# Merging sorted runs by falling-gap stages instead of pairwise rounds, with the gathers put in another order

## The chip, the cores and the metric

The kernel runs on one core of one Trainium2 chip. The metric is the device time of one execution, in microseconds. The engines are named as the profile names them: PE multiplies matrices, DVE is the vector engine, ACT the scalar engine, POOL is GpSimd, SP issues most of the plain transfers.

## The reference

One GraphSAGE layer on a random graph of N = 12,500 nodes, E = 800,000 edges and D = 64 features:

```python
def reference(x, src, dst, deg_inv, w_self, w_neigh):
    N = x.shape[0]
    nsum = _segment_sum(x[src], dst, N)
    h_neigh = nsum * deg_inv[:, None]
    return x @ w_self + h_neigh @ w_neigh
```

## The kernel before

The kernel turns the gather and the segment sum into matrix multiplications with one-hot matrices. For that, edges must stand in buckets: a bucket is a pair of a block of 156 destinations and a block of 128 sources, 7,938 in all.

**Keys and runs.** Each edge becomes one 32-bit key, with its bucket in the upper bits, that is compared as a float. Each of the 128 partitions sorts its own 6,250 keys (`sort_runs`): a stage compares places a fixed gap apart, with one `min` and one `max` on DVE over every second place and a small ACT copy of the unpaired places; the gaps fall from 2601 to 1 (`GAPS`). The last 26 stages are done in three segments, low, middle and high keys.

**Gathering runs.** The sorted keys are written to DRAM. `find_rows` counts in each run where each range of buckets starts (256 counts, on ACT or on DVE by `on_act`). From the starts, POOL gathers with indirect transfers (`gather_runs`, L461): the ranges go to partitions, and each partition then holds 128 short runs, 64 keys wide in part 0 (38 buckets to a partition) and 48 in part 1 (25 buckets). Behind each gather stand one or two small fills on POOL (`pause`, L374).

**Merging.** `merge_runs` merges the 128 runs of a partition pair by pair in seven rounds (`merge_round`, L274 and L286; the last round of part 0 is `merge_last`, L303 and L318), in the order of the gathers: 16, 16, 32 and 64 runs for part 0. `LENS` holds the length that a merged run may have at each level. The last round of part 0 finishes the lower 2,240 places first.

**Windows and decoding.** The merged row goes to DRAM. `count_below` counts for each bucket where it begins, and POOL gathers a window of 186 keys around that place (`gather_window`, L621). For part 0, `find_buckets` counts all 38 buckets while the upper keys are finished, and `gather_buckets` then gathers the 38 windows. `decode_buckets` splits the keys into source and destination numbers (L668 to L673) and collects what does not fit (L707 to L722).

**The node loop.** `nodes` goes over 7,938 buckets in tiles of eight. For each bucket DVE makes two one-hot matrices (`one_hots`, L798 and L801), PE picks features with one (L827), ACT moves them out of PSUM (L837; from tile 503 on DVE takes some, L835), and PE adds them up with the other (L882).

**Order.** From the run sort on, the order is written by hand (`tc.manual_schedule()`): every engine gets its instructions in the order of the Python statements, and each engine's queue is served in order. `merge_runs` is a generator that yields the estimated cost of every DVE instruction, so that other work can be put between. Part 0 is merged before the loop. Part 1 is merged partly in `sums_and_merge` between the steps of the decode of part 0 (2,800 ns to a step), and the rest inside the loop at 320 ns a tile. After it, still inside the loop, part 1 is counted, gathered and decoded.

Of the kernel before, what the change touches and what calls it, by code (L numbers as in the profile page):

```python
# [38 lines left out]
LENS = ((64, 108, 188, 336, 608, 1144, 2176, 4320),  # L39
        (48, 80, 132, 236, 420, 780, 1472, 2912))  # L40
LROW = [l[-1] for l in LENS]
FIRST = 104
EXT = 29
SIDE = H + EXT
PITCH2 = [l + 2 * SIDE for l in LROW]
# [7 lines left out]
SHARED = 100  # L53
# [4 lines left out]
SIGMA = 6.0  # L58
LOWER = 2240
CLOSE = 32  # L60
BEHIND = 6
# [51 lines left out]
NLOWER = sum(lo + n <= LOWER for lo, n in WIN.w2[0])  # L113
NC1 = len(WIN.w1)


def on_act(c):

    return c % 13 in (0, 2, 4, 7, 9, 11) or c < 128 or c >= 128 + SHARED
# [7 lines left out]
def constants():  # L127
# [6 lines left out]
    assert max(lo + 2 * n for lo, n in WIN.w1[:128]) + LENS[0][0] <= SPLITS[1]  # L134
# [4 lines left out]
    for p in range(2):  # L139
# [11 lines left out]
        c2[:, 4] = first + np.arange(128)[:, None] * PITCH2[p]  # L151
# [8 lines left out]


def reach(k, n, total=None):

    i = np.arange(max(n - k, 0))
    m = 2.0 * i + k + 1
    var = m * (total - m) / total if total else m
    i = i[(k + 1.0) ** 2 <= SIGMA ** 2 * var]
    return (int(i[0]), int(i[-1]) + 1) if len(i) else (0, 0)  # L170


def distances(n, total=None):

    out = []
    k = 1
    while k < n:
        lo, hi = reach(k, n, total)
        if hi > lo:
            out.insert(0, (k, lo if lo > 3 else 0, hi))  # L180
        k *= 2
    return out
# [62 lines left out]
def merge_plan(ln, lout):  # L245

    out = []
    c = lout  # L250
    for k, lo, hi in reversed(distances(ln)):
        out.insert(0, (k, lo, min(hi, c // 2), min(hi, (c + 1) // 2 - k)))
        alone = (0, lo + k), (hi + k, (c + 1) // 2), (ln, ln + lo), (ln + hi, ln + c // 2)
        c = min(2 * ln, c + 2 * k - 1)
    return out, (c + 1) // 2, c // 2, [(a, e) for a, e in alone if e > a]


def merge_round(nc, src, oth, off, rstride, nruns, ln, lout, late):

    plan, na, nb, alone = merge_plan(ln, lout)
    n2 = nruns // 2

    def at(t, first, n, step=1):
        return view(t, off + first, [[2 * ln, n2], [step, n]])

    def both():
        for a, e in alone:
            nc.scalar.activation(at(src, a, e - a), at(oth, a, e - a), AF.Copy)  # L270

    for op, n, to in ((OP.min, na, 0), (OP.max, nb, ln)):
        x, y = (view(src, off + o, [[2 * rstride, n2], [1, n]]) for o in (0, rstride))
        nc.vector.tensor_tensor(at(oth, to, n), x, y, op=op)  # L274
        yield n2 * n / 0.96 + 125
    cur, nxt = oth, src
    for j, (k, lo, *ends) in enumerate(plan):
        if not j and not late():
            both()
        for op, end, z in zip((OP.min, OP.max), ends, (1, 2 * k)):  # L280
            n = end - lo
            if k == 1:
                to = at(nxt, 2 * lo + z, n, 2)
            else:
                to = at(nxt, ln + lo if op == OP.min else lo + k, n)
            nc.vector.tensor_tensor(to, at(cur, ln + lo, n), at(cur, lo + k, n), op=op)  # L286
            if not j and op == OP.min and late():
                both()
            yield n2 * n / 0.96 + 125
        cur, nxt = nxt, cur  # L290


def merge_last(nc, src, oth, off, rstride, ln, lout, split, done):


    plan, na, nb, alone = merge_plan(ln, lout)

    def at(t, z, n):
        return view(t, off + z, [[2, n]])
# [11 lines left out]
    for upper in range(2):  # L311
# [10 lines left out]
        if not upper:  # L322
            done(cur)
# [861 lines left out]
```

## Time and profile before

| | |
|---|---|
| time, median of 3 runs | 2043.04 us (2041.74 to 2045.15) |
| profiled execution | 2042.86 us, span 2041.1 us |
| DVE busy | 1862.6 us (91%) |
| ACT busy | 1216.7 us (60%) |
| PE busy | 1001.6 us (49%) |
| POOL busy | 770.4 us (38%) |
| first min of the high segment | 347.4 us |
| last min or max of the merge of part 0 ends | 801.8 us |
| first decode of part 0 | 833.5 us |
| first one-hots of the loop | 930.5 us |
| last merge instruction of part 1 begins | 1402.8 us |

The busy shares are averages over two very different halves. In the first, up to about 930 us, keys are sorted, merged and decoded and PE has almost nothing to do; in the second the node loop runs. A busy share is read within its half.

### The profile page before, as it was taken

Reading aid. Unit: us, or ns where it says so; the run is one execution under the profiler, and the core shown is the slowest. Engines: PE = TensorE matmul, PEld = TensorE weight load, DVE = VectorE, ACT = ScalarE, POOL = GpSimd, SP = SyncE. Lnnn points to the kernel's source line nnn. Section 1 sums busy time; section 2 is a strip of 40 time slices with the busy share of each in tenths; the row PEclk is TensorE's granted clock in tenths of the full one; section 3 lists DMA queues with packets and bytes.
Section 4 is the critical chain, followed back from the end, with each engine's and each line's share of the span. In section 5 each row is a group of like instructions: output and inputs, shape, how many; then the busy total and the mean of one; then the engine's idle time right before and its main releaser. Section 6 shows DMA issues by size and latency. Waiting matters only on the chain.

```text
span 2041.1 us, 56578 instructions
## 1 busy us (share of the span) xinstructions
PE 1001.6 (49%) x24532; PEld 878.6 (43%) x24532; DVE 1862.6 (91%) x2077; ACT 1216.7 (60%) x1802; POOL 770.4 (38%) x973
## 2 busy tenths in 40 slices
PE   0031000000000000005989989998866989989987
PEld 0031000000000000004777878787765878878876
DVE  7999999999999999998999999999998988887885
ACT  6371018470100005224998999998865877877886
POOL 1000000288988898783221321232622123232330
PEclk9976555555555555556999999999987999999998
DMA  4231000011010001217787887888765887887884
GB/s 150 56 89 37 0 26 15 4 50 23 20 19 14 14 10 53 61 43 219 247 273 261 272 256 255 261 265 294 240 208 179 280 266 252 270 275 256 249 264 145
DMA packets 105865, 314.90 MB, mean 154 GB/s; under 512 B 52306, under 2 KB 60340, under 8 KB 104968
## 3 DMA queue, kind: packets, MB, share of 16 engines
q1 hardware_dynamic: 87256, 287.07, 39.9%
q0 software_dynamic: 17776, 22.06, 8.7%
q8 instruction: 193, 3.16, 0.6%
q10 hardware_dynamic: 576, 2.08, 0.3%
q14 instruction: 64, 0.52, 0.1%
HBM read 291.97 MB, written 19.18 MB: 152 GB/s over the span
## 4 chain that ended last, share of the span: by engine, by line
DVE 39%; PE 38%; issue 9%; POOL 7%; ACT 5%; DMA 2%; DVEq 0%; SPq 0%; ACTq 0%; POOLq 0%
PE ct L827 21%; PE acc L882 15%; DVE u L286 11%; DVE a L224 8%; DVE b L224 7%; POOL u L461 4%; DVE u L274 2%; DVE ohd L801 2%; DVE u L318 2%; POOL v L621 2%; DVE ohs L798 2%; ACT xg L837 2%; POOL pad L374 1%; DVE junk L600 1%; PE po L946 1%
## 5 line engine op out<-in xcount | busy, mean ns | idle before, releaser
L837 ACT ACTIVATE xg<-ct 128x1024 f16<-128x1024 f32 (+1 forms) x929 | 877.9, 1051 | 167.2 <-PE ct L827 155.9
L827 PE MATMUL ct<-xh,ohs 128*128 128x128 f16 x7938 | 567.2, 226 | 60.0 <-issue 25.2
L827 PEld LDWEIGHTS <-ohs 128*128 128x128 f16 x7938 | 473.0, 101 | 100.2 <-issue 36.2
L461 POOL DMA_INDIRECT u<-d,ix x256 | 335.4, 1310 | 386.4 <-DVE ix L453 345.3
L286 DVE TENSOR_TENSOR u<-u 128x256 f32<-128x256 f32 (+47 forms) x494 | 452.9, 948 | 23.3 <-ACT u L270 16.2
L882 PE MATMUL acc<-ohd,xg 64*128 64x78 f16 x15876 | 422.1, 201 | 74.8 <-issue 41.8
L882 PEld LDWEIGHTS <-xg 64*128 64x128 f16 x15876 | 337.9, 97 | 144.0 <-issue 64.7
L846 POOL DMA_INDIRECT lx<-xt,lsrc x139 | 232.2, 1671 | 370.0 <-PE acc L862 315.4
L801 DVE TENSOR_TENSOR ohd<-iota,dlT 128x2184 f16<-128x2184 bf16 x284 | 366.3, 1290 | 0.0
L798 DVE TENSOR_SCALAR ohs<-slb,pidx 128x3584 f16<-128x3584 bf16 x284 | 327.4, 1153 | 31.5 <-PE ct L827 28.0
L688 PE MATMUL tr<-idb,l 128*128 128x128 bf16 x63 | 8.6, 278 | 453.2 <-ACT l L682 450.9
L270 ACT ACTIVATE u<-u 128x256 f32<-128x256 f32 (+15 forms) x94 | 46.4, 567 | 283.2 <-DVE u L274 283.1
L688 PEld LDWEIGHTS <-l 128*128 128x128 bf16 x63 | 5.2, 121 | 455.8 <-ACT l L682 454.6
L224 DVE TENSOR_TENSOR a<-b 128x764 f32<-128x764 f32 (+39 forms) x104 | 171.5, 1692 | 3.8
L224 DVE TENSOR_TENSOR b<-a 128x764 f32<-128x764 f32 (+39 forms) x104 | 171.5, 1691 | 3.6
L954 POOL DMA_DIRECT2D out<-o x26 | 25.2, 971 | 351.6 <-DVE o L953 257.9
L835 DVE CAST xg<-ct 128x1024 f16<-128x1024 f32 x70 | 85.6, 1223 | 76.8 <-PE ct L827 76.5
L451 PE MATMUL stp<-idf,st 128*128 128x128 f32 x2 | 0.9, 445 | 283.4 <-DVE st L449 283.4
L451 PEld LDWEIGHTS stp<-idf,st 128*128 128x128 f32 x2 | 0.4, 183 | 283.9 <-issue 283.9
L621 POOL DMA_INDIRECT v<-d,ix x63 | 79.9, 1269 | 76.8 <-ACT ix L651 49.4
L442 ACT ACTIVATE junka<-b,c 128x220 bf16<-128x220 f32 (+42 forms) x202 | 90.1, 446 | 12.0 <-DVE b L224 6.0
L374 POOL MEMSET pad<- 128x93 f32 x454 | 87.7, 193 | 9.4
(140 smaller groups left out, 813.5 us busy)
## 6 DMA issues: line engine op xcount, KB each, us to landing
slb<-sl SPq DMA_DIRECT2D x284, 896.0 KB
u<-d,ix POOLq DMA_INDIRECT x256, 2.7
xt<-xh SPq DMA_DIRECT2D x1, 3136.0 KB
own<-os SPq DMA_DIRECT2D x12, 256.0 KB
fo<-own SPq DMA_DIRECT2D x26, 117.0 KB
out<-o POOLq DMA_DIRECT2D x26, 117.0 KB, 3.4
lx<-xt,lsrc POOLq DMA_INDIRECT x139, 6.8
rd<-dst SPq DMA_DIRECT2D x4, 521.0 KB
```

The source lines that it names most:

```text
L224: nc.vector.tensor_tensor(view(dst, lo + sh, [[st, g], [1, l]]), x, y, op=op)
L286: nc.vector.tensor_tensor(to, at(cur, ln + lo, n), at(cur, lo + k, n), op=op)
L374: self.nc.gpsimd.memset(self.pad, 0.0)
L442: nc.scalar.activation(junks[0][:, :n], w, AF.Sign, bias=self.c1[:, 0, c:c + 1], accum_out=a)
L461: nc.gpsimd.indirect_dma_start(out=u[:nr, p * w:(p + 1) * w], out_offset=None, in_=src, in_offset=bass.IndirectOffsetOnAxis(ap=self.start[ ...
L621: self.nc.gpsimd.indirect_dma_start(out=self.v[:, k].bitcast(F32), out_offset=None, in_=flat(self.d2[part], 128 * PITCH2[part]), in_offset ...
L798: nc.vector.tensor_scalar(s.rearrange("p c s -> p (c s)"), b, self.pidx[:, :1], None, op0=OP.is_equal)
L801: nc.vector.tensor_tensor(d, self.iota[:, None].to_broadcast([128, 14, HN, 2]), ix, op=OP.is_equal)
L827: nc.tensor.matmul(ct[:, i * 128:(i + 1) * 128], cols[i][0], self.xh[:, (b0 + i) % NB].rearrange("p a f -> p (a f)"), start=True, stop=True)
L837: nc.scalar.activation(xg[:, :cnt * 128], ct[:, :cnt * 128], AF.Copy)
L846: nc.gpsimd.indirect_dma_start(out=x, out_offset=None, in_=self.xt, in_offset=bass.IndirectOffsetOnAxis(ap=self.left[p][1][:, c:c + 1], ax ...
L882: nc.tensor.matmul(acc[h][:, db % OCT * HN:(db % OCT + 1) * HN], xg[r, i * 128:(i + 1) * 128], d[r], start=db % OCT == 0 and sb == 0, stop ...
```

## The change

- The seven pairwise rounds go. The runs of a block of 32 are written interleaved, key r of run q at place 32 r + q, and sorted by `near` stages of falling gaps (193 to 31 in part 0, each gap twice); then the four blocks are interleaved and sorted by `far` stages (169 down to 1). A stage is one `min`, one `max` and, where places are unpaired, small ACT copies. `lens` holds how far each stage needs to reach. The blocks are merged as 64, 32 and 32 runs.
- The last 20 stages of part 0 finish the lower 2,240 places first, then the upper ones. The lower 18 windows are counted and gathered while the upper places are sorted, from a DRAM tensor of their own; the other 20 windows come from a second one. Their indices are computed on ACT, one by one.
- The remaining 49 counts of part 0 stand before the high segment instead of between its stages, 27 of them on DVE, and the gathers of part 0 start there, with no pause. Of part 1's counts, 60 instead of 100 stand before the merge; the other 68 come at two of three merge instructions.
- POOL gathers 80 runs of part 1, then the lower windows, 16 more runs, the upper windows, and the last 32 runs. Before it was 104 runs, all windows, 24 runs. The two pauses after each gather of part 1 stay.

```diff
+MERGE = (((193, 133, 89, 65, 51, 31), (169, 131, 73, 49, 31, 27, 15, 13, 9, 7, 5, 3, 3, 1, 1, 1, 1),
+          (2048, 1968, 1816, 1652, 1564, 1464, 1396, 1356, 1320, 1284, 1272, 1256, 5000, 4760, 4672, 4612)),
+         ((225, 133, 71, 59, 53), (201, 109, 55, 49, 31, 23, 19, 15, 13, 9, 5, 5, 3, 3, 1, 1, 1),
+          (1536, 1432, 1380, 1232, 1176, 1088, 1020, 980, 936, 912, 3624, 3392, 3336, 3236, 3196, 3144, 3100)))
+PAUSE = (0, 2)
-FIRST = 104
+FIRST = 80
+THEN = 96
-SHARED = 100
+SHARED = 60
+LAST = 20
...
 def on_act(c):
-    return c % 13 in (0, 2, 4, 7, 9, 11) or c < 128 or c >= 128 + SHARED
+    if c < 128:
+        return c < NEARLY or (c - NEARLY) % 9 in (0, 2, 4, 6)
+    return c >= 128 + SHARED or c % 2 == 0
...
     def gather_runs(self, part, u, runs):
...
-            self.pause(1 if part == 0 and p >= CLOSE else 2)
+            self.pause(PAUSE[part])
...
     def merge_runs(...):
+        def first(b, nb, gap, end):
+            a, rows = gap // 32, end // 32
+            dims = lambda c: [[n, nb], [2 * w, 16], [1, c]]
+            outs = lambda c: [[n, nb], [2, 16], [32, c]]
+            copy(b * n + w, b * n + 1, dims(a), outs(a))
+            copy(b * n + w - a, b * n + 32 * (w - a), dims(rows - w + a), outs(rows - w + a))
+            yield from pair(b * n, b * n + w + a, dims(0), (b * n, (outs(0), min(w - a, rows))),
+                            (b * n + gap, (outs(0), min(w, rows) - a)))
...
+        def stage(b, nb, gap, odd, last, end, low, cut):
+            o = b * n
+            one = lambda c: [[n, nb], [2, c]]
+            inside = gap < EDGE and last == end
+            if not inside:
+                for a, c in (every2(1 - odd, min(gap + odd, end), low, cut),
+                             every2(last - gap + (last - gap - odd) % 2, end, low, cut)):
+                    copy(o + a, o + a, one(c), one(c))
+            a, c = every2(odd, end if inside else min(last - gap, end), low, cut)
+            h, k = every2(1 - odd if inside else gap + odd, end, low, cut)
+            for op, out, x, count in ((OP.min, a, a, c), (OP.max, h, h - gap, k)):
+                d = [[n, nb], [2, count]]
+                if count > 0:
+                    nc.vector.tensor_tensor(view(dst, EDGE + o + out, d), view(src, EDGE + o + x, d),
+                                            view(src, EDGE + o + x + gap, d), op=op)
+                    yield cost(count * nb)
...
     def after_sort(self, es, mps, aps):
...
+            for _ in rows:
+                pass
+            self.gather_runs(0, u0, range(128))
+            for step in high:
                 step()
...
-            for _ in self.merge_runs(0, u[0], other, (16, 16, 32, 64)):
-                if rows and next(rows, None) is None:
+            ways = None
+            for i, _ in enumerate(self.merge_runs(0, u0, other, ((0, 2), (2, 1), (3, 1)))):
+                if rows and (i % 3 != 2) and next(rows, None) is None:
                     rows = None
                     self.l1b.close()
-                    self.gather_runs(1, u[1], range(FIRST))
+                    self.gather_runs(1, u1, range(FIRST))
...
+                if self.lower and not ways:
+                    vp = va.enter_context(tc.tile_pool(name="va", bufs=1, side="right"))
+                    self.windows(0, vp)
+                    self.store_rows(0, sync)
+                    ways = self.find_and_gather(0, range(NLOWER), 1)
+                elif ways and i % 2:
+                    next(ways, None)
+            for _ in ways:
+                pass
+            self.store_rows(1, sync)
+            self.gather_runs(1, u1, range(FIRST, THEN))
...
     def sums_and_merge(...):
+        for _ in self.find_and_gather(0, range(NLOWER, KPRS[0]), 1):
+            pass
+        self.gather_runs(1, u1, range(THEN, 128))
+        merge = self.merge_runs(1, u1, other, ((0, 2), (2, 1), (3, 1)))
         t = 0
         for k in self.decode_buckets(0, self.v, vp, mps):
             t += 2800
             while t > 0 and k < KPRS[0]:
                 t -= next(merge)
```

More of the change, by code (lines that the diff above doesn't have):

```diff
@@ L242, in sort_runs @@
     return cur, segments
[L245 to L290, printed above, removed]
@@ new lines, in merge_runs @@
+        na = 2 * len(near)
+        for b, nb in blocks:
+            src, dst = u, pong
+            for t in range(na):
+                gap, end = near[t // 2], lens[t]
+                if t:
+                    yield from stage(b, nb, gap, t % 2, lens[t - 1], end, 0, n)
+                else:
+                    yield from first(b, nb, gap, end)
+                src, dst = dst, src
+        src, dst = u, pong
+        yield from joined(far[0], lens[na - 1], lens[na])
+        src, dst = dst, src
```

286 lines of the change are left out of this document (112 added, 174 removed).

## The prediction

> **What bounds the kernel now.** I read the busy shares by slice first, then the engines over stretches, then the timelines of DVE and POOL.
>
> ```profile
> span 2041.1 us, 56578 instructions
> ...
> PE   0031000000000000005989989998866989989987
> ...
> DVE  7999999999999999998999999999998988887885
> ...
> POOL 1000000288988898783221321232622123232330
> ```
>
> A slice is 51 us. Up to slice 18 (about 930 us) DVE is full and PE empty: keys are sorted, merged and decoded there. After it PE is full: the node loop. POOL is nearly full in slices 7 to 17, with the gathers of runs and windows.
>
> ```profile
> core 0: us, PE busy (x) PEld busy (x) DVE busy (x) ACT busy (x) POOL busy (x), PEclk, DMA share, GB/s
> 347.40:412.50 65.10, 0.45 (x1) 0.18 (x1) 62.21 (x56) 33.46 (x126) 17.26 (x23) 0.50 0.05 16
> 440.00:801.80 361.80, 0.45 (x1) 0.18 (x1) 341.49 (x386) 53.11 (x146) 322.80 (x509) 0.50 0.09 19
> 833.40:930.50 97.10, 5.87 (x38) 3.24 (x38) 90.37 (x132) 21.45 (x42) 87.15 (x133) 0.50 0.25 66
> 932.00:1400.00 468.00, 417.02 (x10557) 367.40 (x10555) 442.25 (x478) 419.85 (x477) 110.29 (x65) 0.95 0.81 259
> 1400.00:1566.00 166.00, 126.82 (x3039) 110.42 (x3037) 158.53 (x220) 126.89 (x169) 60.24 (x51) 0.89 0.70 232
> 1566.00:2000.00 434.00, 391.00 (x9972) 345.29 (x9974) 360.67 (x401) 339.30 (x369) 118.20 (x78) 0.95 0.82 261
> ```
>
> These are: the high segment of the run sort; the merge of part 0; the decode of part 0; then the loop while part 1 merges, while part 1 is counted and decoded, and afterwards. DVE sets the first three, but POOL is busy for 323 of the 362 us of the merge and 87 of the 97 us of the decode. Whoever shortens DVE's work there meets POOL next. That is my whole forecast: DVE's saving is real and POOL's queue takes it back.
>
> **DVE's prices, and the new merge.**
>
> ```profile
> 392.73 2.42 DVE L224 TENSOR_TENSOR a<-b 128x1057 f32<-128x1057 f32 x2
> 395.19 2.43 DVE L224 TENSOR_TENSOR b<-a 128x1057 f32<-128x1057 f32 x2
> L224 DVE TENSOR_TENSOR a<-b 128x764 f32<-128x764 f32 x26 | 23.7, 952 | 0.4
> L224 DVE TENSOR_TENSOR a<-b 128x3100 f32<-128x3100 f32 x2 | 6.7, 3386 | 0.1
> ```
>
> The last two rows give (3386 - 952) / (3100 - 764) = 1.042 ns an element. The first two start 2.46 us apart for two instructions, so 1.23 us each, 0.13 above the 1.10 of the elements. These stages already step over every second element, as the new merge's do, so the price carries over.
>
> I count instructions from the code. The old plan of part 0 is 370 instructions on 287,188 elements: 299 + 48 = 347 us. A new stage is one min and one max over every second place; the second near stage of part 0 (gap 193, end 1968), for one block, is 927 and 887 elements. Added up, part 0 is: near 72 instructions on 70,544 elements, 83 us; far up to the split 28 on 61,607, 68 us; lower 40 on 45,292, 52 us; upper 40 on 41,108, 48 us. Sum 251 us, 96 less. Part 1 falls from 212 instructions on 193,080 elements (229 us) to 128 on 144,716 (167 us). The ACT copies of unpaired places (up to 226 elements) run beside the stage and cost nothing while ACT is as free as in these stretches (53 of 362 us). In the loop they queue behind ACT's evacuations, and DVE's next stage, and the one-hots behind it, wait for them.
>
> ```profile
> DVE u L286 <- ACT u L270: 16.2, 16, 2.1
> ```
>
> That is the whole of such waiting over 1,200 us of old merges, so I take nothing; if that cover goes, the 30 or so stages with copies at its longest wait of 2.1 are 60 us of DVE, of which the loop, PE-bound, would see a part. The indices that move from DVE to ACT, the edge fills, the third window tensor and the lower windows' counts on ACT lie beside DVE's stages or its waits: nothing.
>
> **POOL's prices.**
>
> ```profile
> 596.18:812.20 216.02, 154.76 (x104) 0.50 0.09 22
> 886.20:930.50 44.30, 30.27 (x24) 0.50 0.21 59
> 823.40:886.20 62.80, 3.65 (x24) 2.07 (x24) 59.53 (x101) 14.91 (x28) 56.81 (x76) 0.50 0.27 69
> 714.00 13.22 DVE L286 TENSOR_TENSOR u<-u 128x1152 f32<-128x1152 f32 x10
> 715.36 2.07 POOL L461 DMA_INDIRECT u<-d,ix  x1 [0.15 <-issue]
> 717.43 0.42 POOL L374 MEMSET pad<- 128x93 f32 x2
> 718.01 2.09 POOL L461 DMA_INDIRECT u<-d,ix  x1 [0.15 <-issue]
> 412.57 0.43 DVE L444 TENSOR_SCALAR_CACHE_REDUCE junkd<-b,c 128x214 bf16<-128x214 f32 x1
> 412.89 0.95 POOL L461 DMA_INDIRECT u<-d,ix  x1 [0.15 <-issue]
> 592.29 0.95 POOL L461 DMA_INDIRECT u<-d,ix  x1 [0.16 <-issue]
> 593.59 0.95 POOL L461 DMA_INDIRECT u<-d,ix  x1 [0.16 <-issue]
> ```
>
> A gather takes 0.95 us beside DVE's counts and 2.07 beside its min and max: in the rows at 714 to 718 DVE's instructions are 1.32 us apart and gathers with two pauses 2.65, two DVE instructions. I read it so: a gather that meets a running min or max goes on only when that ends, and then needs some 0.8 us more. With the two pauses (0.42 and gaps) it has just missed the next boundary, and waits for the one after. So a gather with two pauses costs two DVE instructions (2.4 to 2.6 us) beside stages of 1.2 to 1.3 us, and 0.95 + 0.42 + gaps = 1.53 when DVE stands still. The stretch of 104 such gathers averages 2.08, the last 24 (beside the decode) 1.85. The 38 windows, with one pause, average 62.8 / 38 = 1.65; a pause and its gap are 0.35 (the two last rows start 1.30 apart), so 1.30 without. A gather without pause is in no row. It is at least 0.95 and, by the last two rows, at most 1.30 beside an idle DVE; I take 1.10 (0.95 and one issue gap of 0.15), and beside min and max one per DVE instruction, if that lasts over 1.1 us, else one per two.
>
> **The path to the node loop, in order.** All times are from the start of the span; the old high segment starts at 347.4.
>
> ```profile
> L442 ACT ACTIVATE junka<-b,c 128x220 bf16<-128x220 f32 (+42 forms) x202 | 90.1, 446 | 12.0 <-DVE b L224 6.0
> L442 ACT ACTIVATION_READ_ACCUMULATOR junka<-b,c 128x1 f32 x202 | 38.0, 188 | 0.0
> L444 DVE TENSOR_SCALAR_CACHE_REDUCE junkd<-b,c 128x213 bf16<-128x213 f32 (+50 forms) x54 | 21.5, 398 | 1.9
> ```
>
> 1. The 49 late counts of part 0 now stand before the high segment: 27 on DVE at 0.44 (between the 0.40 of the row and 0.48 with its accumulator read) are 12 us, 22 on ACT at 0.63 are 14, and ACT enters some 1.5 us late. The starts are there at about 365 instead of 392.5, and the high segment runs from 365 to 429 instead of to 412.5.
> 2. The upper counts before the merge fall from 100 to 60, on DVE from 54 to 30: 13 us, to 442.
> 3. The 128 gathers of part 0 run from 365: 52 beside the 52 instructions of the high segment, 12 in the 13 us of counts, so the 64 of the first two blocks have landed at about 444 (2.7 us to landing). A block is a quarter of the near elements, 17,636: the pair of blocks has 24 near instructions of 1,470, 1.66 us each, and ends at 484; 24 more gathers fit. Eight of block 2 are missing: 8 x 1.10, DVE waits 9 us. Block 2 has 24 of 0.89 us and ends at 514; 12 or 13 fit, 19 are missing, DVE waits 20. Block 3 ends at 556.
> 4. Far 68: 623 or 624. Lower to 676, upper to 724. Before: 801.8.
> 5. Here it turns. 60 counts were done up front; the other 68 come at two of three merge instructions, so the starts of part 1 are worked out after the 102nd, two instructions into the lower stages: 626. POOL's queue then gets 80 gathers of part 1 with two pauses, and only behind them the 18 lower windows. Twenty fit beside the lower stages (50 / 2.6), twenty beside the upper (48 / 2.4), the last forty take 1.53: 61 us. They end at 785. The lower windows were to be gathered while the upper keys are sorted; they are ready to, but stand behind these 80.
> 6. DVE's next instruction after the merge is the decode of windows 0 to 3, ahead of any merge of part 1. Four windows at 1.10 and a landing: 792. DVE stands still from 724 to 792, 68 us. Before, that decode began at 833.4, so 41 us are still ahead.
> 7. POOL goes on: 38 windows at 1.30 (49 us) and 48 gathers of part 1, between 1.53 and the 1.85 of the row, at 1.7 (82 us): 916, landed at 919. The merge paced into the decode is 20 steps of 2.8 us; the pair of blocks and block 2 use up 40 of those 56, and then DVE waits for the last run, inside the decode. Behind it lie 17 us of merge, two groups of decode (4) and the last steps (L707 to L722, 10): 950.
>
> ```profile
> 920.24 4.73 DVE L722 MAX8 top<-e 128x8 f32<-128x138 f32 x16
> 930.51 1.17 DVE L798 TENSOR_SCALAR ohs<-slb,pidx 128x3584 f16<-128x3584 bf16 x1 [2.10 <-DMA slb<-sl]
> ```
>
> 8. From the end of the MAX8 at 925.0 to the first one-hot at 930.5 are 5.5 us, and that stays: the loop starts at about 955, 24.5 late.
>
> **The loop.** 24 matmuls of a tile of eight columns: 10,557 in 468 us are 1.064 us a tile while merging, 9,972 in 434 us 1.045 afterwards. The merge costs the loop 2%, since PE is the bound either way. Left at its start are now 66 instructions, 110 us by the code's own cost; at 320 ns a tile that is 343 tiles.
>
> ```profile
> 930.00:1404.00 474.00, 145.04 (x131) 0.95 0.81 260
> L835 DVE CAST xg<-ct 128x1024 f16<-128x1024 f32 x70 | 85.6, 1223 | 76.8 <-PE ct L827 76.5
> ```
>
> Before, 131 instructions last to 1404, some 440 tiles. Ninety-seven tiles at 0.019 less: 2 us. The stretch of counts and decode did 3,039 / 24 = 127 tiles in 166 us, against 132 for them at 1.045: it loses 34 us to DVE, which is busy for 158.5 of it. It keeps its work, but now ends near tile 440, before tile 503, where casts on DVE begin; some eight or nine casts of 1.22 leave it. I take half, 5 us.
>
> **Sum.** The profiled execution took 2042.9 (span 2041.1 and 1.8 around it; the median of the runs is 2043.0). 2042.9 + 24.5 - 2 - 5 = 2060. About 0.2% (4 us) is what a measurement of this kernel can tell from no change.
>
> **Rivals.**
> *Gathers slip through; faster.*
>
> ```profile
> 669.92 6.12 DVE L286 TENSOR_TENSOR u<-u 128x1384 f32<-128x1384 f32 x4
> 671.38 0.96 POOL L461 DMA_INDIRECT u<-d,ix  x1 [0.15 <-issue]
> 672.92 0.95 POOL L461 DMA_INDIRECT u<-d,ix  x1 [0.15 <-issue]
> ```
>
> Here gathers kept DVE's pace of 1.53 and none waited, so the outcome hangs on phase. If the 128 gathers of part 1 average 1.6, step 5 ends at 754 and step 7 at 754 + 42 + 77 + 3 = 876, the loop starts at 912, and with step 3's waits at 10 instead of 29 us at 893: 2042.9 - 37.5 - 7 = 1998. The forecast's own average is (159 + 82) / 128 = 1.88; it takes about 1.75 to cancel the loss (17.5 us / 128 less). Against it: 2.08 over 104.
> *Unpaused gathers crowd out DVE; slower still.* The same lack of pauses could make each gather hold DVE up. At 0.4 us for 128 gathers, or at 1.65 a gather instead of 1.1 to 1.23, step 3 ends 40 to 50 us later and everything behind it: about 2105. For it: nobody has shown them without pause. Against it: DVE's 13.22 us for ten instructions above are 1.32 each, the plain price, with four to five gathers running. The Trainium skill (SBUF — State Buffer, Who interferes with whom) has a VectorE instruction with two SBUF inputs and a GpSimd one that reads SBUF lock each other out, and the first to start blocks the other for its whole length; by its second half each gather could cost DVE up to its 0.95 us, 122 us for part 0, and the sum would be some 2180. The trace agrees that the gather waits; that DVE waits for the gather it does not show.
> *It cancels.* If DVE bounds the loop more than I think (34 us of loss halved, the merging tiles at 1.045), the loop gives back 20 to 25: 2043.
>
> **How the numbers follow.** Forecast (2040 to 2085) 0.50, slip-through (1985 to 2035) 0.25, crowding (2085 to 2125) 0.13, cancelling (2030 to 2047) 0.12. Faster: 0.25, and 0.05 of cancelling and 0.04 of the forecast's low end, 0.34. Same: 0.05 of cancelling and 0.03 of the forecast, 0.08. Slower 0.58. The range 2000 to 2098 leaves out the lower third of slip-through and about the upper two thirds of crowding, 0.17.
>
> **What would show it.** In the profile after: merge instructions of part 0 at 180 and some 251 us; first window gather near 785 behind 80 gathers; DVE idle 60 to 75 us before the first decode, released by POOL; a second long wait of DVE in the decode, for the last runs; first one-hot near 955. I am wrong if windows start under 750, if gathers of part 1 average under 1.7, or if block 3 starts after 560.

## The result, and the profile after

The changed kernel takes 2112.4 us (median of 4 runs, 2102.0 to 2117.4) where the kernel before takes 2042.4 on the same chip: a ratio of 1.0335, 95% interval 1.0288 to 1.0381. It is slower, as forecast, by 70 us instead of 17. The profiled execution took 2116.9 us with a span of 2114.9. First its busy shares by slice.

```profile
span 2114.9 us, 56184 instructions
...
PE   0051000000000000000788989887788998899997
...
DVE  7999999925899950646999999989968887788885
...
POOL 1000001778102988882213213334222132133231
```

A slice is now 53 us. DVE was full from slice 1 to the loop; now it has holes in slices 8 and 9 and again in 14 to 18, and POOL, which was busy from slice 7 to the loop, has next to nothing to do in slices 10 to 12. The stretches give the times and the counts.

```profile
core 0: us, PE busy (x) PEld busy (x) DVE busy (x) ACT busy (x) POOL busy (x), PEclk, DMA share, GB/s
362.00:426.30 64.30, 0.00 (x0) 0.00 (x0) 61.97 (x54) 6.48 (x29) 49.30 (x49) 1.00 0.12 24
426.30:492.30 66.00, 0.00 (x0) 0.00 (x0) 12.71 (x60) 15.44 (x56) 49.95 (x53) 1.00 0.18 49
492.30:550.00 57.70, 0.00 (x0) 0.00 (x0) 42.11 (x25) 12.71 (x55) 39.06 (x27) 1.00 0.08 16
597.00:671.00 74.00, 0.00 (x0) 0.00 (x0) 73.00 (x32) 10.00 (x54) 0.00 (x0) 1.00 0.00 0
771.00:845.00 74.00, 0.00 (x0) 0.00 (x0) 2.94 (x6) 20.12 (x61) 62.24 (x134) 1.00 0.16 42
```

The rows are the high segment, the 60 counts of part 1 behind it, the pair of blocks, the far stages, and the wait for the windows. The high segment is as forecast. In the second row DVE has 12.7 us of work and takes 66 for it. The waits between 424 and 1010 us (engine, tile and line, what it waited for: total, times, longest) name the holes:

```profile
POOL u L382 <- DVE ix L374: 135.0, 1, 135.0
...
ACT junka L363 <- remote: 78.0, 30, 5.1
DVE v L631 <- issue: 71.5, 1, 71.5
...
DVE u L404 <- DMA u<-d,ix: 46.9, 1, 46.9
...
DVE junkd L365 <- remote: 40.4, 17, 3.1
...
DVE junkd L365 <- issue: 11.9, 5, 2.4
```

The 71.5 is the forecast wait for the windows that stand behind 80 gathers, and the 46.9 is the one inside the decode for the last runs. The waits in front of the counts (78.0 on ACT; 40.4 and 11.9 on DVE) were in no forecast. In the first row POOL waits 135 us for the starts of part 1. The timeline shows how the counts go (start, duration, idle time before in brackets), and where two later steps begin.

```profile
482.42 0.94 POOL L382 DMA_INDIRECT u<-d,ix  x1 [0.30 <-issue]
482.47 0.40 DVE L365 TENSOR_SCALAR_CACHE_REDUCE junkd<-b,c 128x181 bf16<-128x181 f32 x1 [2.39 <-remote]
482.80 0.08 DVE L365 DVE_READ_ACCUMULATOR junkd<-b,c 128x1 f32 x1
483.67 0.94 POOL L382 DMA_INDIRECT u<-d,ix  x1 [0.30 <-issue]
483.87 0.45 ACT L363 ACTIVATE junka<-b,c 128x180 bf16<-128x180 f32 x1 [2.26 <-remote]
484.23 0.19 ACT L363 ACTIVATION_READ_ACCUMULATOR junka<-b,c 128x1 f32 x1
484.92 0.94 POOL L382 DMA_INDIRECT u<-d,ix  x1 [0.30 <-issue]
485.27 0.40 DVE L365 TENSOR_SCALAR_CACHE_REDUCE junkd<-b,c 128x179 bf16<-128x179 f32 x1 [2.39 <-remote]
...
841.96 0.69 DVE L631 TENSOR_TENSOR v<-v,c 128x512 int32<-128x512 int32 x1 [71.54 <-issue]
...
1006.32 1.15 DVE L761 TENSOR_SCALAR ohs<-slb,pidx 128x3584 f16<-128x3584 bf16 x1
```

Gathers without a fill follow each other every 1.25 us. DVE begins a count every 2.80 us and ACT one in between: one count in 1.40 us over both, so one instruction in 0.70 on average, since each count has a read of the accumulator behind it. Each engine is idle for over 2.2 us in front of a count of 0.4. The loop begins at 1006.3 (forecast 955) and then takes 1108.6 us to the end of the span, against 1110.6 before.

### The profile page after: what moved, and what is told of

Same layout as the page of the kernel before. It is cut to its first block, busy times and chain, and to the rows that moved or that the text cites. A ratio compares the mean times of both kernels' runs of the same rounds, so it can differ in the third digit from the quotient of the medians.

```text
span 2114.9 us, 56184 instructions
## 1 busy us (share of the span) xinstructions
PE 1010.4 (48%) x24532; PEld 880.8 (42%) x24532; DVE 1725.0 (82%) x1756; ACT 1196.3 (57%) x1872; POOL 696.0 (33%) x778
## 4 chain that ended last, share of the span: by engine, by line
PE 38%; DVE 33%; POOL 11%; issue 10%; ACT 3%; another core or an unknown queue 3%; DMA 2%; DVEq 0%; SPq 0%; ACTq 0%; POOLq 0%
PE ct L790 21%; PE acc L845 15%; DVE a L218 8%; DVE b L218 8%; POOL u L382 8%; DVE u L444 7%; POOL pad L295 2%; DVE ohd L764 2%; DVE ohs L761 2%; ACT xg L800 1%; DVE u L404 1%; PE po L909 1%; DVE junk L590 1%; PE acc L825 1%
## 5 line engine op out<-in xcount | busy, mean ns | idle before, releaser
L382 POOL DMA_INDIRECT u<-d,ix x256 | 301.9, 1179 | 383.4 <-DVE ix L374 324.9
L444 DVE TENSOR_TENSOR u<-u 128x1456 f32<-128x1456 f32 (+46 forms) x292 | 392.8, 1377 | 22.6 <-ACT u L409 9.5
L363 ACT ACTIVATE junka<-b,c 128x132 bf16<-128x132 f32 (+42 forms) x199 | 86.3, 434 | 100.6 <-remote 78.0
L409 ACT ACTIVATE u<-u 128x30 f32<-128x30 f32 (+34 forms) x136 | 29.4, 262 | 150.5 <-DVE u L444 65.1
L594 POOL DMA_INDIRECT v<-d,ix x63 | 75.5, 1199 | 61.6 <-ACT ix L613 46.4
L220 ACT ACTIVATE b<-a 128x1 f32<-128x1 f32 (+21 forms) x52 | 18.2, 381 | 132.6 <-DVE a L218 110.8
```

The costliest lines, as they stand in the source:

```text
L363: nc.scalar.activation(junks[0][:, :n], w, AF.Sign, bias=self.c1[:, 0, c:c + 1], accum_out=a)
L382: nc.gpsimd.indirect_dma_start(out=u[:nr, EDGE + p * w:EDGE + (p + 1) * w], out_offset=None, in_=src, in_offset=bass.IndirectOffsetOnAxis( ...
L444: nc.vector.tensor_tensor(view(dst, EDGE + o + out, d), view(src, EDGE + o + x, d), view(src, EDGE + o + x + gap, d), op=op)
L594: self.nc.gpsimd.indirect_dma_start(out=self.v[:, k].bitcast(F32), out_offset=None, in_=flat(self.d2[home(part, k)], 128 * PITCH2[home(par ...
```

## Experiments

Two theories came out of that. **Theory 1**: a stream of gathers without fills holds up the counts. **Theory P**: POOL's queue, begun when the starts of part 1 are there, sets the start of the loop, whatever DVE does. Theory 2 (every other count on ACT ties the two engines together) and the others stand in the expectations. The expectations count the loop from the wait in front of the first one-hots, up to 3 us before the times given here. In the table a + marks what is added to "one fill, runs inside"; "and a lighter decode" adds to the row above it; the three rows that begin with "before" change the kernel before, and all others the changed kernel. Each kernel ran beside the kernel before, whose median differed from chip to chip, so the ratio is what compares.

| | time | before beside it | ratio, 95% | starts of part 1 | first decode | loop |
|---|---|---|---|---|---|---|
| changed kernel | 2112.4 | 2042.4 | 1.0335 (1.0288 to 1.0381) | 673.8 | 842.0 | 1006.3 |
| one fill, part 0 | 2106.9 | 2054.4 | 1.0273 (1.0239 to 1.0307) | 662.1 | 830.5 | 995.4 |
| old division of counts | 2114.7 | 2054.4 | 1.0299 (1.0260 to 1.0337) | 671.8 | 839.7 | 1004.4 |
| before, no fills in part 0 | 2175.8 | 2054.4 | 1.0616 (1.0569 to 1.0664) | 579.0 | 958.4 | 1055.6 |
| one fill, runs inside | 2096.8 | 2054.4 | 1.0232 (1.0192 to 1.0273) | 658.1 | 826.3 | 989.7 |
| + fills only from run 48 | 2100.5 | 2046.2 | 1.0283 (1.0248 to 1.0317) | 656.3 | 824.5 | 987.6 |
| + early starts of part 1 | 2054.3 | 2046.2 | 1.0026 (0.9995 to 1.0058) | 584.8 | 780.7 | 945.7 |
| + one fill in part 1 | 2037.7 | 2046.2 | 0.9956 (0.9935 to 0.9977) | 661.0 | 783.6 | 934.6 |
| + windows early | 2112.3 | 2046.2 | 1.0324 (1.0280 to 1.0367) | 659.8 | 756.4 | 1002.9 |
| + early starts and one fill | 2002.2 | 2049.4 | 0.9776 (0.9736 to 0.9815) | 586.1 | 758.1 | 892.7 |
| and a lighter decode | 1957.3 | 2049.4 | 0.9563 (0.9527 to 0.9599) | 585.1 | 757.1 | 836.9 |
| eight places for the 0/1 values | 2107.9 | 2049.4 | 1.0281 (1.0229 to 1.0333) | 671.1 | 839.3 | 1004.0 |
| before, one fill everywhere | 2102.8 | 2049.4 | 1.0265 (1.0215 to 1.0314) | 492.2 | 875.6 | 972.2 |
| before, lighter decode | 2029.8 | 2039.3 | 0.9937 (0.9913 to 0.9961) | 453.8 | 833.5 | 905.1 |
| counts of part 1 later | 2107.6 | 2039.3 | 1.0302 (1.0243 to 1.0360) | 691.1 | 840.5 | 1005.3 |

**What holds the counts up.** First one fill back behind the gathers of part 0:

```diff
-PAUSE = (0, 2)
+PAUSE = (1, 2)
```

> One small fill is put back behind each gather of part 0, nothing else is changed. Theory 1 (gathers that follow each other without a fill hold up the counts of ACT and DVE): the 60 counts of the upper starts run at their own pace again (DVE one per 0.48 us, ACT one per 0.61) and take 13 to 20 us from 426 instead of 66; the first interleaving min then waits only for gathers (released by the DMA of u), and begins between 446 and 477; node loop earlier by 15 to 45 us, time 2065 to 2100. Theory 2 (giving every other count to ACT ties the two engines together): the counts go on at one per 1.40 us, the first interleaving min begins near 490, time 2105 to 2120.

The counts run at 0.47 us again and end near 440. But the loop starts only 11 us earlier (15 to 45 were expected), and the time stays above the expected range. The waits of DVE:

```profile
DVE u L404 <- DMA u<-d,ix: 101.7, 4, 47.3
DVE v L631 <- issue: 71.8, 1, 71.8
```

Four waits for runs instead of one: with the fill the last gather of part 0 starts at 558.9 instead of 538.3, and DVE now waits for runs that had landed before while it stood at the counts. Next, no fill, but the old division of counts:

```diff
-    return c >= 128 + SHARED or c % 2 == 0
+    return c >= 128 + SHARED or c % 13 in (0, 2, 4, 7, 9, 11)
```

> The gathers of part 0 keep following each other without a fill; the first 60 counts of part 1 are divided between ACT and DVE by the pattern of the kernel before (6 of 13 on ACT) instead of every other one. Theory 1 (the gathers): still about 1.4 us for each count, over 60 us from 426 to the first interleaving min, time within 10 us of 2112. Theory 2 (the alternation): counts at 0.48 and 0.61 us, the first interleaving min before 480, time under 2100.

```profile
L365 DVE TENSOR_SCALAR_CACHE_REDUCE junkd<-b,c 128x213 bf16<-128x213 f32 (+28 forms) x32 | 13.4, 420 | 57.3 <-remote 46.9 <-issue 9.5 <-DVE junkd L365 0.7
```

DVE's counts, 32 of them here, still start mostly 2.80 us apart and have 57.3 us of idle time before them, and the first interleaving min comes at 497.9: theory 2 falls. Then the old kernel without fills in part 0:

```diff
-            self.pause(1 if part == 0 and p >= CLOSE else 2)
+            self.pause(0 if part == 0 else 2)
```

> The kernel before, with the fills behind the gathers of part 0 taken out; its pairwise merge, its order and its division of the counts stay. Theory 1 (the gathers): the 100 counts after the high segment, which took 24 us from 412, stretch to at least 80 us while the gathers last (128 at 1.25 us from 393, to about 553), the first merge instruction begins after 480, and the time rises by 20 to 70 us to 2065 to 2110. Theory 2 (the alternation): nothing is stretched here, the first merge instruction stays near 436 to 445 and the time within 2030 to 2045.

Its row of counts on DVE (busy time, mean | idle time before them) is:

```profile
L444 DVE TENSOR_SCALAR_CACHE_REDUCE junkd<-b,c 128x213 bf16<-128x213 f32 (+50 forms) x54 | 21.5, 398 | 101.3 <-remote 78.3 <-issue 21.6 <-DVE junkd L444 1.0
```

The same 54 counts of 398 ns that had 1.9 us of idle time now have 101.3. The merge starts at 535.8 instead of 436.8, and the kernel loses over 6%, more than was expected. Part of the rest lies in the merge itself, whose min and max are short at first (0.4 to 0.6 us each). Its rows in the kernel before and in this run:

```profile
L286 DVE TENSOR_TENSOR u<-u 128x776 f32<-128x776 f32 (+42 forms) x385 | 333.1, 904 | 22.5 <-ACT u L270 16.0
```

```profile
L286 DVE TENSOR_TENSOR u<-u 128x448 f32<-128x448 f32 (+43 forms) x324 | 274.4, 888 | 41.1 <-remote 15.6 <-ACT u L270 12.7 <-issue 7.2
```

So it is not counts alone that are held up. The fills of the old kernel were no waste. One fill instead of two does not do there:

```diff
-            self.pause(1 if part == 0 and p >= CLOSE else 2)
+            self.pause(1)
```

> The kernel before with one fill instead of two behind each gather where it had two (the first 32 of part 0 and all 128 of part 1). Theory P holds there too, as far as POOL was the bound: the 104 gathers beside the pairwise merge of part 0, 216 us, take 140 to 170, are done before the merge ends (801.8), windows start near 806 instead of 823 and the last 24 gathers end 5 to 10 us sooner, the loop starts 15 to 25 us earlier; time 0.7 to 1.2% under before. Rival (before was DVE's alone): within 0.2% of before.

```profile
L444 DVE TENSOR_SCALAR_CACHE_REDUCE junkd<-b,c 128x213 bf16<-128x213 f32 (+50 forms) x54 | 21.5, 398 | 30.7 <-remote 13.1 <-DVE junkd L444 11.1 <-issue 5.2
```

A miss with the wrong sign. POOL's gathers did end earlier, but the windows wait for the end of the merge and their counts, and before them the counts lost 29 us of the 42 by which the loop starts late. They run freely for 15 us from 412 and then are held. The 60 counts of the first experiment were done in 14 us, which fits with that. With the fills left out only beside the high segment, where no count runs,

```diff
-            self.pause(PAUSE[part])
+            self.pause(0 if part == 0 and p < 48 else PAUSE[part])
```

> The base is the kernel with one fill behind the gathers of part 0 and the runs inside (2096.8 us; it enters the loop at 986.8 us). Here the first 48 gathers of part 0, which run beside the high segment, follow each other without a fill, the other 80 keep theirs. Theory 1 (what gathers without a fill hold up are the counts): no count is held up, since none runs beside those 48; 48 instead of 40 gathers are done by 426, the last gather of part 0 starts near 545 instead of 558, DVE waits about 10 us less for runs, the loop starts near 977, time 2082 to 2093. Rival (gathers without a fill also hold up the min and max of the high segment): the segment takes over 66 us instead of 64 and nothing is won, 2095 or more.

the segment keeps its 64 us, yet the 30 counts behind it, beside gathers with a fill, are held up. Their rows in the kernel with one fill and runs inside and in this run:

```profile
L365 DVE TENSOR_SCALAR_CACHE_REDUCE junkd<-b,c 128x213 bf16<-128x213 f32 (+28 forms) x30 | 12.6, 420 | 1.1
```

```profile
L365 DVE TENSOR_SCALAR_CACHE_REDUCE junkd<-b,c 128x213 bf16<-128x213 f32 (+28 forms) x30 | 12.6, 420 | 33.3 <-remote 21.6 <-DVE junkd L365 9.0 <-issue 2.4
```

The forecast of theory 1 missed here: the held state outlasts the gathers that bring it about. The last gather without a fill starts at 426.6, and the counts are held from 429 on, where the same gathers with fills had let them pass. Even POOL's fills now wait, up to 1.5 us. How long the state would last without the gathers with fills, which held counts by themselves in the run before, this run does not show. Eight places instead of one for what the counts write and nobody reads:

```diff
-        junks = [l1.tile([128, 512], BF, name=f"junk{e}") for e in "ad"]
+        junks = [[l1.tile([128, 256], BF, name=f"junk{e}{i}") for i in range(8)] for e in "ad"]
...
+            junk = junks[e][turn[e] % 8]
+            turn[e] += 1
```

> The changed kernel, part 0 without fills, but the counts write the 0/1 values that nobody reads to eight places in turn instead of one, so that a count waits for the end of the eighth before it and not of the last. Theory L (what gathers without a fill hold up is the news that the engine's own last count has ended, late by about 1 us each): the counts run at 0.48 and 0.61 us again and take 13 to 25 us from 426 instead of 66; the interleaving min then waits for runs and begins near 450; time 2095 to 2110. Theory T (such news come at a limited rate, one in 1.4 us over both engines): a few more counts pass at first and then it is one per 1.4 us again, first interleaving min after 475, time 2105 to 2118.

```profile
455.83 0.47 ACT L367 ACTIVATE junka<-b,c 128x191 bf16<-128x191 f32 x1 [1.20 <-ACT junka L367]
455.84 0.41 DVE L369 TENSOR_SCALAR_CACHE_REDUCE junkd<-b,c 128x190 bf16<-128x190 f32 x1 [1.31 <-DVE junkd L369]
456.30 0.94 POOL L386 DMA_INDIRECT u<-d,ix  x1 [0.30 <-issue]
457.24 0.20 ACT L367 ACTIVATION_READ_ACCUMULATOR junka<-b,c 128x1 f32 x1 [0.94 <-issue]
457.26 0.08 DVE L369 DVE_READ_ACCUMULATOR junkd<-b,c 128x1 f32 x1 [1.01 <-issue]
...
458.63 0.46 ACT L367 ACTIVATE junka<-b,c 128x189 bf16<-128x189 f32 x1 [1.19 <-issue]
```

Theory L falls: a count no longer waits for the last one, and still there are four instructions in 2.80 us over both engines; the accumulator reads now wait too. The pace is that of theory T, but not one message at a time: an ACT and a DVE instruction begin within 0.02 us of each other, such a pair every 1.40 us. In the changed kernel, too, the starts of the held instructions of both engines (45 of them between 430 and 492 us) lie on one grid of 0.70 us, each within 0.05 us of it. So the engines are let go at common moments, and one instruction in 0.70 us is what that comes to on average. Last, all counts moved away from the gathers without fills:

```diff
-SHARED = 60
+SHARED = 0
...
-                if rows and (i % 3 != 2) and next(rows, None) is None:
+                if rows and i >= 72 and (next(rows, None) is None or next(rows, None) is None):
```

> The changed kernel, gathers of part 0 without fills; none of the 128 counts of part 1 runs beside them: all are on ACT, two at every merge instruction from the first far stage on. Theory 1 (a stream of gathers without fills lets ACT and DVE together begin only one instruction in 0.70 us; longer instructions do not notice): the first interleaving min begins at 448 to 452 instead of 492, the pair of blocks takes its plain 40 to 45 us, the third block ends at 555 to 570 instead of 597, the merge of part 0 at 728 to 745 instead of 769. Theory P (the time hangs on when POOL gets the starts of part 1, here again near 675 to 690): all that gain is lost again in front of the windows of part 0, the loop starts at 1000 to 1020, time within 10 us of 2112. Rival (DVE's earlier merge carries through): time under 2095. Rival to theory 1 (these gathers hold up the min and max too): block 3 ends no earlier than 590.

The stretch of the pair of blocks and DVE's longest waits:

```profile
448.00:492.00 44.00, 0.00 (x0) 0.00 (x0) 40.80 (x24) 3.85 (x17) 36.69 (x25) 0.50 0.09 19
```

```profile
DVE u L404 <- DMA u<-d,ix: 101.1, 4, 47.1
DVE v L631 <- issue: 97.3, 1, 97.3
```

Both theories hold at once. The first interleaving min comes at 446.9, the pair takes its plain 44 us beside 25 gathers without fills (and with no counts in ACT's queue), block 3 ends at 569.4 (596.6 in the changed kernel) and the merge at 743.2 instead of 770.4. None of these 27 us arrive: the starts of part 1 are there at 691, the wait for the windows grows from 71.5 to 97.3, and the loop starts at 1005.3.

**POOL's queue.** These runs have one fill in part 0 and the runs inside (below). First the counts of part 1 at every merge instruction:

```diff
-                if rows and (i % 3 != 2) and next(rows, None) is None:
+                if rows and next(rows, None) is None:
```

> Same base. The 68 late counts of part 1 come at every merge instruction instead of two of three, so that the starts of part 1 are there after 68 merge instructions, near 580 us, and not at 658. Theory P (POOL's queue of 80 gathers, 38 windows and 48 gathers, begun when the starts of part 1 are there, sets the start of the loop; POOL had nothing to do from 559 to 658): 80 gathers beside far, lower and upper stages are done near 767, the first windows are read by DVE near 772 instead of 826, the loop starts near 933, time 2035 to 2055. Rival D (DVE's own work and the runs of part 0 set it): the first decode moves by under 15 us, time 2085 to 2100.

The starts come 73 us earlier, the loop 44. The wait for the windows was 71.6 us and is now:

```profile
DVE v L632 <- issue: 24.2, 1, 24.2
```

Then one fill instead of two in part 1:

```diff
-PAUSE = (1, 2)
+PAUSE = (1, 1)
```

> Same base. One fill instead of two behind the gathers of part 1. Theory P, with a gather costing as many DVE instructions as it meets: with one fill it is ready again before the next stage instruction (1.27 us) ends, so it costs one and not two, 80 gathers take about 105 us instead of 159, the first decode comes near 768 instead of 826, the loop near 917, time 2020 to 2040. Rival: beside these stages a gather costs two instructions whatever the fill, and only the part beside an idle DVE gains 0.2 us a gather: loop 970 to 980, time 2080 to 2092.

The 80 gathers start between 661.5 and 775.3, 1.44 us apart, instead of 2.0. The loop starts 55 us earlier, though the starts come no sooner. Then the windows ahead of most runs:

```diff
-FIRST = 80
-THEN = 96
+FIRST = 20
+THEN = 20
```

> Same base. POOL gathers 20 runs of part 1, then all 38 windows of part 0, then the other 108 runs (instead of 80, lower windows, 16, upper windows, 32). Theory P as the sum of the queue: the first decode comes straight after the merge, near 756 instead of 826, but the queue is as long as before, its last runs land near 955, DVE waits for them inside the decode instead, the loop starts within 10 us of 987 and the time is 2087 to 2105. Rival W (the windows standing behind 80 gathers are themselves the loss): the loop starts 60 to 70 us earlier, time 2025 to 2040.

```profile
DVE u L405 <- DMA u<-d,ix: 204.1, 6, 97.9
```

The first decode comes 70 us earlier, straight behind the merge. All of it is paid back inside the decode, where DVE now waits 97.9 us for the first 64 runs of part 1; the loop is 13 us later still (10 were expected at most) and the time above its range. Another order of the same queue gained nothing, where a shorter queue in the run before gained 55 us. Both winning edits together:

```diff
-                if rows and (i % 3 != 2) and next(rows, None) is None:
+                if rows and next(rows, None) is None:
...
-PAUSE = (1, 2)
+PAUSE = (1, 1)
```

> The kernel with the runs inside, the counts of part 1 at every merge instruction, and one fill behind every gather of both parts: the two edits that won, together. Theory P (POOL's queue sets the start of the loop): starts of part 1 near 585, 80 gathers at 2.4 us beside the far stages and 1.27 beside the others done near 722, the first decode straight after the merge near 757, the last run landed near 845, the loop starts near 880; time 1975 to 2000. Rival D (with that DVE is the bound again, whose instructions have not become fewer): the loop starts no earlier than 915 and the time is 2015 or more.

The first decode comes straight behind the merge and the loop at 892.7; the time is 2 us over what theory P gave, and 13 under the least that rival D allowed. Behind the merge DVE now waits only inside the decode, 23.2 us for the last runs and 14.5 for ACT's copies. With a lighter merge in the decode:

```diff
-            t += 2800
+            t += 1400
...
-                t += 320
+                t += 400
```

> As the one before, and the merge of part 1 is paced at 1400 instead of 2800 ns to a decode step and 400 instead of 320 ns to a tile of the loop. Theory P: DVE does not reach the last block of runs inside the decode, stands for no gather there, the loop starts at 830 to 855, and the loop, PE-bound, takes back 10 to 20 us of it; time 1960 to 1990. Rival D (the loop while merging is as much DVE's as PE's): what leaves the decode comes back in the loop, time within 8 us of the kernel before it.

This one is 4.4% faster than the kernel before, 3 us under its expected range. The wait of 23.2 us for the last runs is gone and less merge stands in the decode, so the loop starts 56 us earlier: once the queue is ahead, what DVE does sets the start of the loop again, and the "whatever DVE does" of theory P holds no longer. Its stretch from the end of the merge of part 0 to the loop:

```profile
755.00:834.00 79.00, 5.85 (x38) 3.21 (x38) 65.12 (x98) 41.15 (x111) 68.00 (x80) 1.00 0.25 73
```

In the changed kernel 236 us lie between the two, here 80, and DVE works in 65 of the 79 shown. From the first one-hots to the end are 1116 us, 8 more than in the changed kernel: that is what the loop takes back. The same paces in the kernel before:

> The kernel before with the paces of the fastest kernel so far (1400 instead of 2800 ns of merge to a decode step, 400 instead of 320 to a tile of the loop), nothing else. Theory M (the gain of that kernel rests on the shorter merge and the order of POOL's queue together with the pace): the old kernel leaves about 28 us of merge out of the decode, starts its loop near 902, and with 212 instructions of 229 us to spread the loop takes most of it back; time between 20 us under and 5 us over before. Rival (the pace alone is the gain): 35 us or more under before.

That gives 0.6%, as theory M has it, so the pace alone is a small part.

**The price of the interleaving writes.** In the instructions that write the runs interleaved the inner step was turned from keys to runs (the same places read and written):

```diff
                 d[-1][1] = od[-1][1] = count
+                d[-2:], od[-2:] = d[:-3:-1], od[:-3:-1]
```

> The kernel with one fill, and in the interleaving instructions (first and joined) the inner step goes over the runs instead of the keys: each write lands 8 bytes behind the one before (16 for joined: only pairs lie 8 apart), each read 512 bytes (for joined: two blocks) away. The same places are read and written. If the step between writes sets the price, first falls from 3.28 us for 1856 elements to 1.95 to 2.1 and from 1.65 to about 1.0 for 928, some 8 us in all on the way to the loop; if a far step costs the same on the reading side, the 3.28 stays; if both sides cost, it rises over 3.5.

By form, in the changed kernel and in this one (busy, mean ns | idle):

```profile
L404 DVE TENSOR_TENSOR u<-u 128x928 f32<-128x928 f32 x4 | 6.6, 1742 | 0.0
...
L404 DVE TENSOR_TENSOR u<-u 128x2428 f32<-128x2428 f32 x1 | 4.5, 4460 | 0.1
```

```profile
L405 DVE TENSOR_TENSOR u<-u 128x928 f32<-128x928 f32 x4 | 6.8, 1746 | 35.1 <-DMA u<-d,ix 35.1
...
L405 DVE TENSOR_TENSOR u<-u 128x2428 f32<-128x2428 f32 x1 | 2.7, 2743 | 0.1
```

In the second row (the first far stage) the writes move from 16 to 8 bytes apart and the reads alternate between two places 16 KB apart: the price falls from 1.84 to 1.13 ns an element, where a plain min or max of 2,380 elements costs 1.11 (2640 ns). In the first row (the first near stage) the writes move from 128 to 8 bytes apart, but the reads go round sixteen places, 512 bytes apart: it stays at 1.88, where a plain one of 927 elements costs 1.21 (1126 ns). So writes 16 bytes or more apart, and reads that go round sixteen far places, each cost some 0.7 ns; reads that alternate between two far places do not. The Trainium skill (Advanced Engine Details and Errata, Memory Cachelines) says that an access wants two hits in a 16-byte line and pays for a new line each time. The writes and the reads over sixteen places agree; the reads that alternate do not, since they change line each time and pay nothing. The sizes are measured here.

## Why the prediction was wrong

The direction was right, and so was the part of the mechanism that puts POOL's queue in front of the windows and the last runs; but DVE saved less to begin with, since the merge ended at 770.4 instead of 724 (801.8 before). The size came out as 70 us instead of 17, outside the range (2000 to 2098). By its steps:

1. Starts of part 0 at 361.8 (forecast 365), high segment to 426.3 (429): right.
2. **The step that failed.** The 60 counts were priced at 13 us, from rows in which gathers had fills behind them; they took 66. The price of a gather without a fill was bounded by its own time on POOL, 1.10 (measured 1.25), and the bound never asked what it does to short instructions elsewhere. (The two rows at 592.29 and 593.59 that gave the bound of 1.30 "beside an idle DVE" were misread: six min and max ran beside them.)

```profile
589.73 7.81 DVE L286 TENSOR_TENSOR u<-u 128x1053 f32<-128x1053 f32 x6
```

The rival of crowding came nearest in size (2105), but at the wrong place: it had the min and max held up. Those of the new merge and the high segment are not, as the 64 us of the high segment and the 44 of the pair in the last run show; the counts and their accumulator reads are.
3. No waits of 9 and 20 us for runs, since all had come while DVE stood. But the pair of blocks took 57.5 us instead of 42: ACT's copies of unpaired places, priced at nothing, stand in its queue behind counts that are held up, and DVE waited 9.5 us for them, 3.0 for the counts themselves and 2.7 for what the profile does not name. Block 3 ended at 596.6 instead of 556. With the counts moved away it ended at 569.4, behind waits of 21.4 (where the counts had stood), 10.1 and 22.4 us: the last two are near the forecast.
4. Merge instructions of part 0, busy time in the changed kernel:

```profile
L444 DVE TENSOR_TENSOR u<-u 128x2160 f32<-128x2160 f32 (+51 forms) x172 | 234.6, 1406 | 20.1 <-ACT u L409 9.5 <-ACT junka L363 3.0 <-remote 2.7
L404 DVE TENSOR_TENSOR u<-u 128x928 f32<-128x928 f32 (+3 forms) x8 | 21.9, 2820 | 0.5 <-issue 0.4
```

180 instructions and 256.5 us, against 251. The merge is as short as worked out, but for the far steps of the eight interleaving ones, 21.9 us where 12,268 plain elements would be 13.8. The far stages took 74 us instead of 68, the lower and upper ones 99 instead of 100.
5. The starts of part 1 came at 673.8 instead of 626, and this is nearly the whole error: 48 us of 51. Against the forecast they are 53 for the counts, 15.5 for the pair, 4 for the other two blocks and 7 for the stages behind them, less 3 for the high segment and less the 29 of waits that did not come. From there all went as written: 161 us from the first of the 80 gathers to the first window (forecast 159).
6. DVE stood 71.5 us for the windows (68).
7. The second wait, 46.9 us, ended at 969.5 instead of 919, for the same 50 us.
8. The loop started at 1006.3 instead of 955. The loop gave back 2 us and not 7. The measured terms, 2042.9 + 75.8 - 2.0, add up to 2116.7, as they must, being differences of the two spans; the profiled execution took 2116.9. The 75.8 are the forecast 24.5 and the 51 of the steps above.

One of its own signs of being wrong came true: block 3 started at 573.2, after 560. What the prediction did not see is that mending step 2 alone gives almost nothing. In the chain the starts of part 1 are tied to a number of merge instructions, and POOL idles 135 us until they come. The counterfactuals part the two: with the counts moved away but late starts, 27 us of DVE's time are won and lost again; with early starts, 44 us arrive in the kernel with one fill and runs inside.

## What to carry to other kernels

When two engines work in turns on one queue, ask when the queue's next batch of work is released and not only how long it is: here counts placed a little earlier were worth 44 us, and a merge 27 us shorter nothing. A filler instruction in a tuned kernel may be paying for something on other engines; before taking it out, look at the shortest instructions that run beside it. For a two-input fp32 vector instruction, price writes 16 bytes or more apart, or reads that go round many far places, at about 1.6 times the plain element, as the two forms here showed.

## What the runs showed of the hardware

Gathers by indirect transfer that follow each other every 1.25 us let DVE and ACT together begin only one short instruction in 0.70 us on average, at moments on one grid of 0.70 us for both engines, after some 3 us in which they still run freely; with a fill of 0.2 us behind each it took 15 us in the old kernel before the counts were held. Min and max of over 1.2 us did not suffer (52 in 64 us beside 49 gathers), nor did those of 0.9 us in block 2 of the run with the counts later (22 of them with 1.1 us of idle time in all); those of 0.4 to 0.6 us in the old kernel's merge did. The Trainium skill (SBUF — State Buffer, Who interferes with whom) has DVE instructions with at most one SBUF input, outside the two-port modes, free of GpSimd, and ACT waiting for nobody. The counts have one such input, apart from the threshold, and all the same they waited: 53 us of idle time before 30 of them on DVE, 78 us on ACT. Whether SBUF is what they waited for no run here shows, so this does not refute the rule. Its rule for two-input instructions, that they shut out a GpSimd instruction that reads SBUF, agrees with gathers of 2.07 beside 0.95 us, if a gather counts as such a reader; the other half, DVE shut out by a gather, no run here shows. What the held instructions wait for, the runs do not show either: it is neither the division between the engines nor the wait of a count for the one before, it outlasts the gathers that bring it about, and it lets both engines go at the same moments.
